# Decode block with a cached attention: value rows from TensorE to GpSimd, key rows from GpSimd to VectorE, and another way to a head's maximum

## The chip, the cores and the metric

The kernel runs on one core of a Trainium2 chip. The metric is the device time of one execution in microseconds; the time of a kernel is the median of several executions. Before the change it is 1319.39 us, the median of three (1319.2 to 1319.57).

## What is computed

One decode step: four sequences (B = 4), one new token each, width D = 512, 32 heads of 128, a key and a value cache of 4096 positions per head and sequence, then a feed-forward layer of width 1792. All is float32.

```
mod = (silu(c) @ w_mod) -> sa, ca, ga, sb, cb, gb          # 6 vectors of 512 per sequence
h = layernorm(x) * (1 + ca) + sa
q = (h @ wq) as [4, 32, 1, 128]
scores = q . k_cache * 128 ** -0.5                          # [4, 32, 1, 4096]
o = softmax(scores) . v_cache
x = x + ga * (o @ wo)
h = layernorm(x) * (1 + cb) + sb
x = x + gb * (silu(h @ w1) @ w2)
```

The two caches hold 268 MB each. They are read once, and nearly all bytes that the kernel moves are theirs.

## The kernel before, in words

The attention is cut into 32 tiles, numbered n = 0 to 31. A tile is four heads (HP = 4) of one sequence: t = n // 4 is the group of heads, b = n % 4 the sequence. Each of the 128 partitions holds 128 consecutive positions of one head (32 partitions per head), so a key tile and a value tile are 128 x 128 x 128 elements each, 8.39 MB: 128 partitions by 128 "rows" (positions) of 128 elements. A tile fills one whole slot of the pool `kv`, which has three slots; the weights that come first (`wm`, `wq`) and last (`wo`, `w12`) use the same three slots. SyncE's queue issues all loads (L86), in the order k1, v0, k2, v1, k3, v2, and so on; a load is issued when its slot is free. With three slots, the load of v(n) goes into the slot of k(n) and waits until the scores of tile n are finished; the load of k(n+2) goes into the slot of v(n-1) and waits until the values of tile n-1 are used up. The order on every engine is the order of the code (a manual schedule).

The loop over n does, for a tile in the middle:

- keys: each key row is multiplied by the query (L283). VectorE does rows 32 to 127 with the query copy `qb`, which lies in PSUM; GpSimd does rows 0 to 31 (`NA` = 32) with the copy `qw` in SBUF, which ScalarE makes (L278). VectorE then sums the 128 elements of each row (L288), its own 96 rows first and GpSimd's 32 after. That gives the 128 x 128 scores `sc`. In tiles 0 and 1 GpSimd has 56 rows (`NL`).
- values of the tile before, n-1: `vmult` and `pv`. GpSimd multiplies rows 0 to 47 (`NP`) by their weights (L331), ScalarE multiplies rows 48 to 55 one at a time (L330, eight instructions), and GpSimd folds these 56 rows (`NV`) to four by four additions (L335, of 28, 12, 8 and 4 rows). TensorE takes rows 56 to 127 unweighted, four rows to a matmul, 18 matmuls, with the weights spread into the stationary operand `pz` (L356). `vsum` (L341) adds GpSimd's four folded rows with one more matmul, read out of the value slot itself.
- maximum: `rowmax` (L292) takes the maximum of each partition's scores; `bmax` (L296) has TensorE transpose it, spread over 128 columns, into PSUM; `negmax` (L301, L302, L304) takes the maximum of each head's 32 columns, multiplies with a mask of -1 (`hn`), and sums. `softexp` has ScalarE take the exponentials (L310), and GpSimd spreads them into `pz` (L316).
- every fourth tile or so VectorE collects a finished group of heads: `gather` (L367, L373), `norm` and `spread`.

On TensorE `vsum(n-1)` stands behind `bmax(n)`. Tiles 30 and 31 have no GpSimd part on their values (`first` gives 0): TensorE takes all 128 rows. At the end come the output projection and the feed-forward, whose weights are loaded behind the last value tile (wo into the slot of k31, w12 into that of v30); small filler matmuls (`busy`) lie between.

Of the kernel before, what the change touches and what calls it, by code (L numbers as in the profile page):

```python
# [9 lines left out]
F32 = mybir.dt.float32  # L10
AF = mybir.ActivationFunctionType
ALU = mybir.AluOpType
AX = mybir.AxisListType
# [4 lines left out]
def kernel(  # L18
# [10 lines left out]
    nc = tc.nc  # L29
    P = 128  # L30
    B, H, S, Dh = kc.shape
# [3 lines left out]
    W = P // G  # L35
    HP = 4
    QW = P // HP
# [6 lines left out]
    JJ = 4  # L44
# [4 lines left out]
    NK = D // P  # L49
    NI = F // P  # L50
    FG = F // G
    NA = 32
    NL = 56
    NV = 56
    NP = 48
    SCALE = 1.0 / math.sqrt(Dh)
    EPS = 1e-5
    N = B * NT
    SLOT = NJ * Dh

    const = ctx.enter_context(tc.tile_pool(name="const", bufs=1))
    kv = ctx.enter_context(tc.tile_pool(name="kv", bufs=3))
    work = ctx.enter_context(tc.tile_pool(name="work", bufs=2))
# [3 lines left out]
    def psum(shape, tag, bufs):  # L67
        return ps.tile(shape, F32, tag=tag, name=tag, bufs=bufs)
# [15 lines left out]
    def fetch(t, src, *cuts):  # L84
        for lo, hi in zip(cuts, cuts[1:]):
            nc.sync.dma_start(t[:, lo:hi], src[:, lo:hi])  # L86

    kt, vt = {}, {}
# [7 lines left out]
    def load_k(n, *cuts):  # L96
        load(kt, kc, "k", n, *cuts)

    def load_v(n):
        load(vt, vc, "v", n)  # L100
# [22 lines left out]
    ident = const.tile([P, P], F32, name="ident")  # L123
# [11 lines left out]
        nc.vector.tensor_scalar(avg[:, g, :], sel, 1.0 / G, None, op0=ALU.mult)  # L135
    hm = const.tile([P, HP], F32, name="hm")
    nc.vector.tensor_reduce(hm, i4, axis=AX.X, op=ALU.add)
    hn = const.tile([P, HP], F32, name="hn")
    nc.vector.tensor_scalar(hn, hm, -1.0, None, op0=ALU.mult)
    jm = const.tile([P, JJ], F32, name="jm")  # L140
    nc.vector.tensor_reduce(jm, ident.rearrange("p (k j) -> p j k", j=JJ), axis=AX.X, op=ALU.add)
    xm = const.tile([P, B], F32, name="xm")
# [15 lines left out]
    hs = const.tile([P, W + E], F32, name="hs")  # L158
# [87 lines left out]
    for k in range(NK):  # L246
        for ch in range(H * Dh // CW):
            i, g = divmod(ch, G)
# [7 lines left out]
    for i in range(2):  # L256
        for u in range(HP):
            o = ZB - QW * u - G * B * i
# [9 lines left out]
    def make_qb(n):  # L268
        if n % B == 0:
            m = work.tile([P, B, Dh], F32, tag="o", name=f"qm{n}", bufs=1)  # L270
            for b in range(B):
                nc.scalar.activation(m[:, b, :], qn, AF.Copy, scale=sel[:, n + b : n + b + 1])  # L272
            p = psum([P, B, Dh], "q", 2)
            nc.tensor.matmul(p, blk.rearrange("p i x -> p (i x)"), m, start=True, stop=True)  # L274
            for b in range(B):
                qb[n + b] = p[:, b, :]
        qw[n] = work.tile([P, Dh], F32, tag="qw", name=f"qw{n}")
        nc.scalar.activation(qw[n], qb[n], AF.Copy)  # L278

    sc, nm, po, rs = {}, {}, {}, {}  # L280

    def mult(eng, src, n, lo, hi):
        eng.tensor_mul(  # L283
            kt[n][:, lo:hi, :], kt[n][:, lo:hi, :], src[n].unsqueeze(1).to_broadcast([P, hi - lo, Dh])
        )

    def red(n, lo, hi):
        nc.vector.tensor_reduce(sc[n][:, lo:hi], kt[n][:, lo:hi, :], axis=AX.X, op=ALU.add)  # L288

    def rowmax(n):  # L290
        nm[n] = work.tile([P, 1], F32, tag="rm", name=f"rm{n}")
        nc.vector.tensor_reduce(nm[n], sc[n], axis=AX.X, op=ALU.max)  # L292

    def bmax(n):
        p = psum([P, P + HP], "mx", 2)
        nc.tensor.transpose(p[:, :P], nm[n].to_broadcast([P, P]), ident)  # L296
        nm[n] = p

    def negmax(n):
        m = nm[n][:, P:]  # L300
        nc.vector.tensor_reduce(m, nm[n][:, :P].rearrange("p (i x) -> p i x", i=HP), axis=AX.X, op=ALU.max)  # L301
        nc.vector.tensor_mul(m, m, hn)  # L302
        nm[n] = work.tile([P, 1], F32, tag="nm", name=f"nm{n}")
        nc.vector.tensor_reduce(nm[n], m, axis=AX.X, op=ALU.add)  # L304

    def softexp(n):
        t, b = divmod(n, B)
        if b == 0:
            rs[t] = work.tile([P, B], F32, tag="rs", name=f"rs{t}")
        nc.scalar.activation(sc[n], sc[n], AF.Exp, bias=nm[n], accum_out=rs[t][:, b : b + 1])  # L310
        for h in range(2):
            f = min(max(first(n) - HG * h, 0), HG)
            m = HG - f
            if not m:
                continue
            nc.gpsimd.tensor_mul(  # L316
                pz[h][:, f * W : HG * W].rearrange("p (g x) -> p g x", g=m)[:, :, E:].rearrange("p g (i j) -> p g i j", i=HP),
                sc[n][:, JJ * (HG * h + f) : HG * JJ * (h + 1)].rearrange("p (g j) -> p g j", j=JJ)
                .unsqueeze(2).to_broadcast([P, m, HP, JJ]),
                hm.unsqueeze(1).unsqueeze(3).to_broadcast([P, m, HP, JJ]),  # L320
            )

    def first(n):
        return NV // JJ if n < N - 2 else 0

    def vmult(n):
        if first(n):
            v = vt[n]
            for j in range(NP, NV):
                nc.scalar.activation(v[:, j, :], v[:, j, :], AF.Copy, scale=sc[n][:, j : j + 1])  # L330
            nc.gpsimd.tensor_mul(  # L331
                v[:, :NP, :], v[:, :NP, :], sc[n][:, :NP].unsqueeze(2).to_broadcast([P, NP, Dh])
            )
            for m, lo in ((28, 28), (12, 16), (8, 8), (JJ, JJ)):
                nc.gpsimd.tensor_add(v[:, :m, :], v[:, :m, :], v[:, lo : lo + m, :])  # L335

    def vsum(n):
        t, b = divmod(n, B)
        q, a = divmod(b, 2)
        o = (1 - a) * E  # L340
        nc.tensor.matmul(  # L341
            po[t, q][0:W, :], hs[:, o : o + W], vt[n][:, :JJ, :].rearrange("p j d -> p (j d)"),
            start=False, stop=a == 1,
        )

    def pv(n):
        t, b = divmod(n, B)
        q, a = divmod(b, 2)
        if a == 0:
            po[t, q] = psum([P, JJ * Dh], "po", 2)  # L350
        f = first(n)
        for j in range(f, NG):
            g = j % G
            h, u = divmod(j, HG)
            o = u * W + (1 - a) * E
            nc.tensor.matmul(  # L356
                po[t, q][W * g : W * (g + 1), :],
                pz[h][:, o : o + W],
                vt[n][:, JJ * j : JJ * (j + 1), :].rearrange("p j d -> p (j d)"),
                start=(a == 0 and j < f + G), stop=(a == 1 and j >= NG - G and (g > 0 or not f)),  # L360
            )
# [25 lines left out]
    def sums(t):  # L387
        p = psum([P, B], "mx", 2)
        if t < TA:
            nc.tensor.matmul(p[W * t : W * (t + 1)], b8.rearrange("p i x -> p (i x)"), rs[t], start=True, stop=True)  # L390
        else:
            nc.tensor.matmul(p, blk.rearrange("p i x -> p (i x)"), rs[t], start=True, stop=True)
        rd[t] = p
# [53 lines left out]
    for n in range(N):  # L447
        t, b = divmod(n, B)
        if n + 1 < N:
            load_k(n + 1)  # L450
        else:
            load_v(n)
        if t and b == 1:
            sums(t - 1)
        sc[n] = work.tile([P, NJ], F32, tag="sc", name=f"sc{n}")
        w, m = (NJ // 2, NL // 2) if n == 0 else (NJ, NL) if n == 1 else (NJ, NA)
        for lo in range(0, NJ, w):
            mult(nc.gpsimd, qw, n, lo, lo + m)
            mult(nc.vector, qb, n, lo + m, lo + w)
            if n + 1 < N and not lo:  # L460
                make_qb(n + 1)
            if n:
                vmult(n - 1)
                pv(n - 1)
            red(n, lo + m, lo + w)
        for lo in range(0, NJ, w):
            red(n, lo, lo + m)
        if n + 1 < N:
            load_v(n)
        else:  # L470
            so = Slot("wo")
            wat, wot = so.take(RA, D), so.take(NT - TA, R, D)
            fetch(so.t, wo, 0, RA * D, SLOT - R * D, SLOT)
            s2 = Slot("w12")
            w1t = s2.take(NK, F)
            w2t = s2.take(NI, D)
            fetch(s2.t, w12, 0, 3 * F, *(NK * F + i * D for i in (0, 5, 8, 10, 11, 12, 13, 14)))
        rowmax(n)
        bmax(n)
        if n and first(n - 1):  # L480
            vsum(n - 1)
        negmax(n)
        softexp(n)
        if b == 3:
            gather(t, 0)
        if n == N - 1:
            sums(t)
            norm(t)
        if t and b == 1:
            gather(t - 1, 1)  # L490
            norm(t - 1)
        if t and b == 2:
            spread(t - 1)
# [25 lines left out]
    for g in range(G):  # L519
        o = g % 2 * P  # L520
# [71 lines left out]
```

## Time and profile before

| | |
|---|---|
| median of three runs | 1319.39 us |
| the profiled execution's own time | 1318.86 us |
| its span, first to last instruction | 1317.0 us |
| bytes read from HBM | 567.30 MB |
| VectorE (DVE) busy | 1045.5 us |
| GpSimd (POOL) busy | 1080.1 us |
| TensorE (PE) matmuls busy | 359.7 us |
| ScalarE (ACT) busy | 125.8 us |
| mean granted TensorE clock | 0.617 of full speed |

The profile is one execution on the chip. A group of instructions is named by its line in the kernel, its engine and operation, and what it writes and reads (partitions x elements); behind the bar stand its busy time, the mean of one in ns, and the engine's idle time just before it with what ended that. The chain of work is followed back from the last instruction to what released each step. A row of the timeline gives start and length in us. "DMA share" is the mean busy share of the core's 16 DMA engines.

### The profile page before, as it was taken

How to read it: one execution, taken by the hardware profiler on the slowest of the kernel's cores; microseconds unless marked ns; L12 is line 12 of the kernel's file. 1: busy time of each engine (PE TensorE's matmuls, PEld its weight loads, DVE VectorE, ACT ScalarE, POOL GpSimd, SP SyncE). 2: the span in 40 equal slices, each digit the busy share in tenths (PEclk: the TensorE clock that was granted, in tenths of full speed). 3: DMA queues.
4: the chain of work that ended last, by engine and by line, in shares of the span. 5: the costliest groups of instructions: out<-in, count | busy, mean ns of one | idle time of the engine just before them, and what ended most of it. 6: DMA issues, size and time to landing. Idle time of an engine off the chain costs nothing.

```text
span 1317.0 us, 5073 instructions
## 1 busy us (share of the span) xinstructions
PE 359.7 (27%) x1756; PEld 95.2 (7%) x1756; DVE 1045.5 (79%) x357; ACT 125.8 (10%) x408; POOL 1080.1 (82%) x257
## 2 busy tenths in 40 slices
PE   3301322221222232122322122132312213221258
PEld 1100000000000000000000000000000000000013
DVE  2597788988878998788898888789887878978762
ACT  1100110010001101011100100000100010000001
POOL 0459888888988888998888899888889888888910
PEclk9856666656666665666665566666556666655669
DMA  9999999999999999999999999999999999999998
GB/s 415 440 420 444 428 435 434 426 442 434 430 440 428 438 435 428 438 434 432 430 442 432 430 439 432 434 434 430 438 432 432 438 432 434 436 432 438 428 426 349
DMA packets 11433, 567.63 MB, mean 431 GB/s; under 512 B 1280, under 2 KB 1296, under 8 KB 2192
## 3 DMA queue, kind: packets, MB, share of 16 engines
q1 hardware_dynamic: 11408, 567.31, 99.6%
q8 instruction: 14, 0.23, 0.1%
q14 instruction: 11, 0.09, 0.0%
HBM read 567.30 MB, written 0.01 MB: 431 GB/s over the span
## 4 chain that ended last, share of the span: by engine, by line
DMA 50%; DVE 27%; POOL 19%; PE 2%; issue 1%; ACT 0%; SPq 0%; DVEq 0%; POOLq 0%
DMA k<-in_A_k_cache_dram 23%; DMA v<-in_A_v_cache_dram 21%; DVE sc L288 16%; DVE k L283 11%; POOL v L335 11%; POOL v L331 8%; DMA w<-in_B_w_dram 3%; DMA wq<-in_A_wq_dram 3%; PE po L341 1%; PE q L249 1%; PE mx L259 0%; ACT qm L272 0%; PE q L274 0%; SPq L86 0%; PE od L378 0%
## 5 line engine op out<-in xcount | busy, mean ns | idle before, releaser
L288 DVE TENSOR_REDUCE sc<-k 128x96 f32<-128x12288 f32 (+3 forms) x66 | 553.1, 8422 | 4.1
L283 DVE TENSOR_TENSOR k<-k,q 128x12288 f32<-128x12288 f32 (+2 forms) x33 | 408.3, 12372 | 183.1 <-DMA k<-in_A_k_cache_dram 168.1
L335 POOL TENSOR_TENSOR v<-v 128x3584 f32<-128x3584 f32 (+1 forms) x120 | 443.8, 3698 | 9.4
L331 POOL TENSOR_TENSOR v<-v,sc 128x6144 f32<-128x6144 f32 x30 | 313.8, 10460 | 103.4 <-DMA v<-in_A_v_cache_dram 103.4
L283 POOL TENSOR_TENSOR k<-k,qw 128x4096 f32<-128x4096 f32 (+2 forms) x33 | 296.4, 8982 | 31.4 <-ACT qw L278 31.4
L356 PE MATMUL po<-v,pz 128*32 128x512 f32 x1208 | 216.3, 839 | 335.6 <-DMA v<-in_A_v_cache_dram 335.6
L341 PE MATMUL po<-v,hs 128*32 128x512 f32 x60 | 57.4, 1061 | 413.8 <-POOL v L335 413.8
L330 ACT ACTIVATE v<-v,sc 128x128 f32<-128x128 f32 x240 | 73.6, 389 | 199.3 <-DMA v<-in_A_v_cache_dram 199.3
L356 PEld LDWEIGHTS po<-v,pz 128*32 128x32 f32 x1208 | 56.1, 148 | 500.8 <-issue 482.3
L296 PE MATMUL mx<-ident,rm 128*128 128x128 f32 x32 | 12.7, 396 | 175.7 <-DVE rm L292 175.7
L278 ACT ACTIVATE qw<-q 128x128 f32<-128x128 f32 x32 | 8.9, 278 | 525.6 <-DVE k L283 424.0
L316 POOL TENSOR_TENSOR pz<-sc,hm 128x32 f32<-128x32 f32 (+1 forms) x64 | 26.7, 438 | 30.4 <-ACT sc L310 30.4
L310 ACT ACTIVATE sc<-sc,nm 128x128 f32<-128x128 f32 x32 | 12.9, 402 | 367.9 <-DVE nm L304 367.9
L341 PEld LDWEIGHTS po<-v,hs 128*32 128x32 f32 x60 | 5.4, 140 | 421.5 <-POOL v L335 421.5
L301 DVE TENSOR_REDUCE mx<-mx 128x4 f32<-128x128 f32 x32 | 9.6, 300 | 17.8 <-PE mx L296 17.8
L367 DVE TENSOR_TENSOR o<-po,jm 128x512 f32<-128x512 f32 x16 | 10.9, 681 | 13.6 <-PE po L356 13.6
L296 PEld LDWEIGHTS mx<-ident,rm 128*128 128x128 f32 x32 | 5.2, 163 | 203.9 <-issue 162.1
L373 DVE TENSOR_REDUCE s<-o 128x128 f32<-128x512 f32 x16 | 16.5, 1034 | 0.6
L274 PE MATMUL q<-qm,blk 128*128 128x512 f32 x16 | 15.6, 1073 | 1.7 <-ACT qm L272 1.7
L200 PE MATMUL q<-wm 128*32 128x512 f32 x48 | 8.9, 668 | 18.9 <-DVE wm L184 18.9
L190 POOL COPY wm<-wm 128x16 f32<-128x16 f32 x1 | 0.2, 212 | 16.0 <-DMA wm<-in_head_dram 16.0
L499 PE MATMUL q<-mod,ident 128*128 128x512 f32 (+2 forms) x24 | 10.7, 554 | 0.0
(114 smaller groups left out, 164.9 us busy)
## 6 DMA issues: line engine op xcount, KB each, us to landing
k<-in_A_k_cache_dram SPq DMA_DIRECT2D x2, 4096.0 KB, 51.1
wm<-in_head_dram SPq DMA_DIRECT2D x1, 6160.0 KB, 17.7
wo<-in_A_wo_dram SPq DMA_DIRECT2D x1, 4096.0 KB, 18.1
wo<-in_A_wo_dram SPq DMA_DIRECT2D x1, 3072.0 KB, 25.0
w<-in_B_w_dram SPq DMA_DIRECT2D x1, 2688.0 KB, 33.1
w<-in_B_w_dram SPq DMA_DIRECT2D x1, 1280.0 KB, 37.3
wo<-in_A_wo_dram SPq DMA_DIRECT2D x1, 1024.0 KB, 27.0
w<-in_B_w_dram SPq DMA_DIRECT2D x4, 256.0 KB, 17.6
```

The source lines that it names most:

```text
L249: nc.tensor.matmul(pq[i][W * g : W * (g + 1), :], hT[:, k, :], wqt[:, k, ch * CW : (ch + 1) * CW], start=k == 0, stop=k == NK - 1,)
L274: nc.tensor.matmul(p, blk.rearrange("p i x -> p (i x)"), m, start=True, stop=True)
L283: eng.tensor_mul(kt[n][:, lo:hi, :], kt[n][:, lo:hi, :], src[n].unsqueeze(1).to_broadcast([P, hi - lo, Dh]))
L288: nc.vector.tensor_reduce(sc[n][:, lo:hi], kt[n][:, lo:hi, :], axis=AX.X, op=ALU.add)
L296: nc.tensor.transpose(p[:, :P], nm[n].to_broadcast([P, P]), ident)
L316: nc.gpsimd.tensor_mul(pz[h][:, f * W : HG * W].rearrange("p (g x) -> p g x", g=m)[:, :, E:].rearrange("p g (i j) -> p g i j", i=HP), sc[n ...
L330: nc.scalar.activation(v[:, j, :], v[:, j, :], AF.Copy, scale=sc[n][:, j : j + 1])
L331: nc.gpsimd.tensor_mul(v[:, :NP, :], v[:, :NP, :], sc[n][:, :NP].unsqueeze(2).to_broadcast([P, NP, Dh]))
L335: nc.gpsimd.tensor_add(v[:, :m, :], v[:, :m, :], v[:, lo : lo + m, :])
L341: nc.tensor.matmul(po[t, q][0:W, :], hs[:, o : o + W], vt[n][:, :JJ, :].rearrange("p j d -> p (j d)"), start=False, stop=a == 1,)
L356: nc.tensor.matmul(po[t, q][W * g : W * (g + 1), :], pz[h][:, o : o + W], vt[n][:, JJ * j : JJ * (j + 1), :].rearrange("p j d -> p (j d)") ...
L373: nc.vector.tensor_reduce(s, o.rearrange("p j d -> p d j"), axis=AX.X, op=ALU.add)
```

## The change

Three things, in one diff.

1. `NV` goes from 56 to 64 and `NP` goes away: GpSimd weighs 64 value rows in one multiplication, ScalarE's eight multiplications are gone, and four additions fold 64 rows as 32, 16, 8 and 4. The last addition writes a tile of its own (`vs`, one buffer), and `vsum` reads that and no longer the value slot. TensorE has 16 matmuls per tile in place of 18. Tile 30 gets 32 rows on GpSimd (`NU`), tile 31 none.
2. `NA` goes from 32 to 8: GpSimd multiplies 8 key rows, VectorE 120, from tile 2 on.
3. `bmax` is gone. `negmax` has VectorE transpose the row maxima in blocks of 32 x 32, take the maximum over 32 columns, and negate it with a `tensor_scalar` of one element per partition, SBUF to SBUF. The mask `hn` is gone.

```diff
-    NA = 32
+    NA = 8
     NL = 56
-    NV = 56
-    NP = 48
+    NV = 64
+    NU = 32
...
-    def bmax(n):
-        p = psum([P, P + HP], "mx", 2)
-        nc.tensor.transpose(p[:, :P], nm[n].to_broadcast([P, P]), ident)
-        nm[n] = p
-
     def negmax(n):
-        m = nm[n][:, P:]
-        nc.vector.tensor_reduce(m, nm[n][:, :P].rearrange("p (i x) -> p i x", i=HP), axis=AX.X, op=ALU.max)
-        nc.vector.tensor_mul(m, m, hn)
-        nm[n] = work.tile([P, 1], F32, tag="nm", name=f"nm{n}")
-        nc.vector.tensor_reduce(nm[n], m, axis=AX.X, op=ALU.add)
+        m = work.tile([P, QW], F32, tag="hx", name=f"hx{n}")
+        nc.vector.transpose(m, nm[n].to_broadcast([P, QW]))
+        nm[n] = work.tile([P, 2], F32, tag="nm", name=f"nm{n}")
+        nc.vector.tensor_reduce(nm[n][:, 0:1], m, axis=AX.X, op=ALU.max)
+        nc.vector.tensor_scalar(nm[n][:, 1:2], nm[n][:, 0:1], -1.0, None, op0=ALU.mult)
...
-        nc.scalar.activation(sc[n], sc[n], AF.Exp, bias=nm[n], accum_out=rs[t][:, b : b + 1])
+        nc.scalar.activation(sc[n], sc[n], AF.Exp, bias=nm[n][:, 1:2], accum_out=rs[t][:, b : b + 1])
...
     def first(n):
-        return NV // JJ if n < N - 2 else 0
+        return (NV if n < N - 2 else NU if n < N - 1 else 0) // JJ
 
     def vmult(n):
-        if first(n):
-            v = vt[n]
-            for j in range(NP, NV):
-                nc.scalar.activation(v[:, j, :], v[:, j, :], AF.Copy, scale=sc[n][:, j : j + 1])
-            nc.gpsimd.tensor_mul(
-                v[:, :NP, :], v[:, :NP, :], sc[n][:, :NP].unsqueeze(2).to_broadcast([P, NP, Dh])
-            )
-            for m, lo in ((28, 28), (12, 16), (8, 8), (JJ, JJ)):
-                nc.gpsimd.tensor_add(v[:, :m, :], v[:, :m, :], v[:, lo : lo + m, :])
+        v, m = vt[n], JJ * first(n)
+        nc.gpsimd.tensor_mul(v[:, :m, :], v[:, :m, :], sc[n][:, :m].unsqueeze(2).to_broadcast([P, m, Dh]))
+        vs[n] = work.tile([P, JJ, Dh], F32, tag="vs", name=f"vs{n}", bufs=1)
+        while m > JJ:
+            m //= 2
+            nc.gpsimd.tensor_add(vs[n] if m == JJ else v[:, :m, :], v[:, :m, :], v[:, m : 2 * m, :])
 
     def vsum(n):
...
-            po[t, q][0:W, :], hs[:, o : o + W], vt[n][:, :JJ, :].rearrange("p j d -> p (j d)"),
+            po[t, q][0:W, :], hs[:, o : o + W], vs[n].rearrange("p j d -> p (j d)"),
...
         rowmax(n)
-        bmax(n)
-        if n and first(n - 1):
+        if n:
             vsum(n - 1)
```

The line numbers of the changed kernel differ: its L281 is L283 of before, L286 is L288, L290 is L292, L309 is L316, L321 is L331, L325 is L335, L331 is L341, L346 is L356.

The order of GpSimd's instructions around the values of tile 6 (`v6`) and the key rows of tile 7 (`k7`); `sc` are scores or weights, `qw` the query. Before:

```order
L316 TENSOR_TENSOR pz0_113<-sc6_598,hm_96 128x2x16
L316 TENSOR_TENSOR pz1_114<-sc6_598,hm_96 128x16x16
L283 TENSOR_TENSOR k7_596<-k7_596,qw7_601 128x4096
L331 TENSOR_TENSOR v6_636<-v6_636,sc6_598 128x6144
L335 TENSOR_TENSOR v6_636<-v6_636 128x3584
L335 TENSOR_TENSOR v6_636<-v6_636 128x1536
L335 TENSOR_TENSOR v6_636<-v6_636 128x1024
L335 TENSOR_TENSOR v6_636<-v6_636 128x512
```

And GpSimd's order at the same place now, with `vs6` as the new tile for the folded rows:

```order
L309 TENSOR_TENSOR pz1_112<-sc6_539,hm_96 128x16x16
L281 TENSOR_TENSOR k7_537<-k7_537,qw7_542 128x1024
L321 TENSOR_TENSOR v6_568<-v6_568,sc6_539 128x8192
L325 TENSOR_TENSOR v6_568<-v6_568 128x4096
L325 TENSOR_TENSOR v6_568<-v6_568 128x2048
L325 TENSOR_TENSOR v6_568<-v6_568 128x1024
L325 TENSOR_TENSOR vs6_598<-v6_568 128x512
```

The small key multiplication stands where the large one stood, the value multiplication and the first two additions are longer, and one of the two spreads into `pz` is gone.

VectorE's order for the scores and the maximum of tile 6, up to the next tile's keys (`mx` lies in PSUM, `od` too, `v`/`oa` belong to the collection of a finished group). Before:

```order
L288 TENSOR_REDUCE sc6_598<-k6_528 128x96
L288 TENSOR_REDUCE sc6_598<-k6_528 128x32
L292 TENSOR_REDUCE rm6_638<-sc6_598 128x1
L301 TENSOR_REDUCE mx_640<-mx_640 128x4
L302 TENSOR_TENSOR mx_640<-mx_640,hn_98 128x4
L304 TENSOR_REDUCE nm6_645<-mx_640 128x1
L416 TENSOR_TENSOR v_650<-od_466,ra_593 32x512
L420 TENSOR_REDUCE oa_130<-v_650 32x64
L283 TENSOR_TENSOR k7_596<-k7_596,q_412 128x12288
```

And VectorE's order there now, with `hx` as the transposed maxima:

```order
L286 TENSOR_REDUCE sc6_539<-k6_480 128x120
L286 TENSOR_REDUCE sc6_539<-k6_480 128x8
L290 TENSOR_REDUCE rm6_570<-sc6_539 128x1
L294 STREAM_TRANSPOSE hx6_573<-rm6_570 128x32
L296 TENSOR_REDUCE nm6_575<-hx6_573 128x1
L297 TENSOR_SCALAR nm6_575<-nm6_575 128x1
L406 TENSOR_TENSOR v_580<-od_429,ra_534 32x512
L410 TENSOR_REDUCE oa_128<-v_580 32x64
L281 TENSOR_TENSOR k7_537<-k7_537,q_386 128x15360
```

Three instructions still stand between the row maxima and the collection, but nothing in them comes from TensorE any more, and the last of them is the `TENSOR_SCALAR` of one element.

More of the change, by code (lines that the diff above doesn't have):

```diff
@@ L137 @@
     nc.vector.tensor_reduce(hm, i4, axis=AX.X, op=ALU.add)
-    hn = const.tile([P, HP], F32, name="hn")
-    nc.vector.tensor_scalar(hn, hm, -1.0, None, op0=ALU.mult)
     jm = const.tile([P, JJ], F32, name="jm")
@@ L278, in make_qb @@
         nc.scalar.activation(qw[n], qb[n], AF.Copy)
-    sc, nm, po, rs = {}, {}, {}, {}
+    sc, nm, po, rs, vs = {}, {}, {}, {}, {}
     def mult(eng, src, n, lo, hi):
```

## The prediction, made blind

> **What bounds the kernel now.** The profile's page comes first: busy time of the engines, the queue's share of the DMA engines, and the shares of the chain that ended last.
>
> ```profile
> PE 359.7 (27%) x1756; PEld 95.2 (7%) x1756; DVE 1045.5 (79%) x357; ACT 125.8 (10%) x408; POOL 1080.1 (82%) x257
> q1 hardware_dynamic: 11408, 567.31, 99.6%
> DMA 50%; DVE 27%; POOL 19%; PE 2%; issue 1%; ACT 0%; SPq 0%; DVEq 0%; POOLq 0%
> ```
>
> The chain gives half to DMA and nearly half to VectorE and GpSimd, as if their work paced the kernel. The queue's row says otherwise: packets occupied the 16 DMA engines for 99.6% of the span, and only 0.4% of 1317.0 us, 5.3 us, was empty. So I read one turn of the chain in order of time, and three tiles in the windows (columns: length, busy time and instructions of PE, PEld, DVE, ACT, POOL, then TensorE clock, DMA share, GB/s).
>
> ```profile
> 571.62 27.38 DMA v<-in_A_v_cache_dram
> 599.13 10.47 POOL v L331
> ...
> 624.75 1.93 PE po L341 x2
> 626.74 30.76 DMA k<-in_A_k_cache_dram
> 657.58 12.97 DVE k L283
> 670.66 17.29 DVE sc L288 x2
> 687.97 27.43 DMA v<-in_A_v_cache_dram
> ```
> ```profile
> 1121.84:1237.62 115.78, 28.39 (x123) 7.61 (x123) 96.04 (x28) 9.89 (x34) 104.36 (x25) 0.59 1.00 435
> ```
>
> The turn is a slot's life: load values, use them, load keys, use them. A load "takes" 27 to 31 us there, but three tiles move six loads of 8.39 MB in 115.78 us, 19.3 us for each at 435 GB/s with a DMA share of 1.00. So a load spends 8 to 11 us queued behind the one before. A tile lasts 38.6 us because two loads last that long. The compute pieces in the chain only decide how early a load joins the queue. The spare time is best seen in the timeline: a value load's issue beside the landing of the key load ahead of it, and a value landing.
>
> ```profile
> 726.61 0.33 SPq L86 DMA_DIRECT2D v<-in_A_v_cache_dram  x1
> ```
> ```profile
> 734.82 12.96 DVE L283 TENSOR_TENSOR k<-k,q 128x12288 f32<-128x12288 f32 x1 [4.45 <-DMA k<-in_A_k_cache_dram]
> ```
> ```profile
> 637.73 10.46 POOL L331 TENSOR_TENSOR v<-v,sc 128x6144 f32<-128x6144 f32 x1 [3.46 <-DMA v<-in_A_v_cache_dram]
> ```
>
> The value load joins at 726.61 and the keys ahead of it land by 734.82: a lead of 8.2 us. The key load of 626.74 (chain above) joins 11.0 us before the values ahead of it land, by 637.73. VectorE waits 4.45 us for its keys in this tile, and 168.1 us over the 30 tiles (group row below), 5.6 on average; GpSimd waits 3.46.
>
> **The change part by part.** The groups, shapes kept apart:
>
> ```profile
> L283 DVE TENSOR_TENSOR k<-k,q 128x12288 f32<-128x12288 f32 x30 | 388.6, 12954 | 168.1 <-DMA k<-in_A_k_cache_dram 168.1
> L288 DVE TENSOR_REDUCE sc<-k 128x96 f32<-128x12288 f32 x30 | 388.6, 12953 | 4.0
> L331 POOL TENSOR_TENSOR v<-v,sc 128x6144 f32<-128x6144 f32 x30 | 313.8, 10460 | 103.4 <-DMA v<-in_A_v_cache_dram 103.4
> L283 POOL TENSOR_TENSOR k<-k,qw 128x4096 f32<-128x4096 f32 x30 | 265.5, 8852 | 0.0
> L335 POOL TENSOR_TENSOR v<-v 128x3584 f32<-128x3584 f32 x30 | 232.0, 7733 | 2.4
> L288 DVE TENSOR_REDUCE sc<-k 128x32 f32<-128x4096 f32 x30 | 132.3, 4409 | 0.0
> L335 POOL TENSOR_TENSOR v<-v 128x1536 f32<-128x1536 f32 x30 | 103.0, 3434 | 2.4
> L335 POOL TENSOR_TENSOR v<-v 128x1024 f32<-128x1024 f32 x30 | 70.7, 2356 | 2.4
> L335 POOL TENSOR_TENSOR v<-v 128x512 f32<-128x512 f32 x30 | 38.1, 1269 | 2.4
> L316 POOL TENSOR_TENSOR pz<-sc,hm 128x256 f32<-128x256 f32 x34 | 20.8, 614 | 16.2 <-ACT sc L310 16.2
> ```
>
> *Keys.* VectorE's product grows by 24 rows: 12.95 us x 120/96 = 16.19, so +3.24 us per tile, +97 us over 30 tiles. The sums cover 128 rows as before: 12.95 x 120/96 + 4.41 / 4 = 17.29 against 17.36. The key slot comes free 3.2 us later, and the value load's lead falls from 8.2 to 5.0 us. What hides it is the key load still in the queue ahead. The lead needed is an issue's start-up; the nearest row is the output's whole transfer, 1.8 us from issue to landing (quoted under the ends), so between 0 and 1.8 us. 5.0 covers it. Were the cover gone, each tile would pay the missing part.
>
> *Values on GpSimd.* The product: 10.46 x 64/48 = 13.95 us. The additions: 7.73 x 32/28 = 8.84, 3.43 x 16/12 = 4.58, 2.36 and 1.27, together 17.05. From landing to the last addition that is 31.0 us and four gaps of 0.07 (the chain's steps), 31.3. Before, the next key load was issued 27.6 us after the values' start (599.13 to 626.74), TensorE's 1.93 included; now the folded rows leave the slot, and that matmul no longer holds it. The key load joins 3.7 us later, with a lead of 11.0 - 3.7 = 7.3 us. A wide product no trace shows: at the additions' pace (7.73 / 3584 an element) it would be 17.7 us, and the lead still 3.5. I take 13.95, the same operation's row.
>
> *GpSimd in all.* Keys 8.85 / 4 = 2.21, values 31.0, one spread 0.61: 33.8 us, against 8.85 + 10.46 + 14.79 + 0.61 and the small second spread, 34.7 without that. It gets about 1 us shorter and keeps waiting for its values. With the wide product at its upper bound it has 37.6, still under 38.6. Eight ScalarE multiplications and two matmuls per tile go from engines busy 10% and 27%; worth nothing.
>
> *The maximum.* Five rows of VectorE's timeline, with what GpSimd runs meanwhile:
>
> ```profile
> 919.23 7.73 POOL L335 TENSOR_TENSOR v<-v 128x3584 f32<-128x3584 f32 x1
> ```
> ```profile
> 920.68 0.30 DVE L301 TENSOR_REDUCE mx<-mx 128x4 f32<-128x128 f32 x1 [0.63 <-PE mx L296]
> 921.02 0.17 DVE L302 TENSOR_TENSOR mx<-mx,hn 128x4 f32<-128x4 f32 x1
> 921.22 0.16 DVE L304 TENSOR_REDUCE nm<-mx 128x1 f32<-128x4 f32 x1
> 921.30 0.34 DVE L423 TENSOR_SCALAR on<-od,rd 128x128 f32<-128x128 f32 x1
> 921.68 0.31 DVE L427 STREAM_TRANSPOSE ot<-on 128x128 f32<-128x128 f32 x1
> ```
>
> The old way costs 0.63 of waiting and 0.63 of work. The new one: a transpose of 32 columns, at most the 0.31 of 128; a reduction between 0.16 and 0.30; a negation near 0.16. That is 0.7 against 1.26, about 0.5 us saved. VectorE's wait for keys in the tightest tile becomes 4.45 - 3.24 + 0.5 = 1.7 us. It stays positive, so VectorE stays ahead of DMA, though it is now the tightest engine. The negation's upper end is a rival, below.
>
> *Ends.* Rows of SyncE's timeline, the output's issue (us to landing last), TensorE's start on the last two value tiles, and the chain's last load:
>
> ```profile
> 0.74 0.38 SPq L118 DMA_DIRECT2D wm<-in_head_dram  x1
> ...
> 1268.01 1.28 SPq L86 DMA_DIRECT2D wo<-in_A_wo_dram  x3
> ```
> ```profile
> out_dram<-end SPq DMA_DIRECT2D x1, 8.0 KB, 1.8
> ```
> ```profile
> 1257.00 9.15 PE L356 MATMUL po<-v,pz 128*32 128x512 f32 x64 [11.11 <-DMA v<-in_A_v_cache_dram]
> ...
> 1276.53 4.50 PE L356 MATMUL po<-v,pz 128*32 128x512 f32 x20 [4.54 <-DMA v<-in_A_v_cache_dram]
> ```
> ```profile
> 1302.47 10.75 DMA w<-in_B_w_dram
> ```
>
> The output weights' load would be issued at 1268.0 + 3.2 = 1271.2 us, 5.3 before the last values land at 1276.5. Tile 30's 32 rows cost GpSimd 6.97 (half of 13.95), 8.21 of additions (4.58, 2.36, 1.27) and gaps, 15.4 us, from 1257.0 to 1272.4; the feed-forward weights wait for that slot, but stand behind 8.39 MB of output weights, 19.3 us, in any case. The end is the landing of their last piece at 1302.47 + 10.75 = 1313.2 us, and 1317.0 - 1313.2 = 3.8 us of last steps that the change doesn't touch. The first load starts at 0.74 as before.
>
> *Sum.* Every added microsecond lies under the queue: 0 on the span. 1317.0 + 0 gives 1317.0, and 1318.9 for the profiled execution (1318.86, span plus 1.86); the median of the runs is 0.53 above that, so 1319.4.
>
> **The rivals.** *The negation waits for GpSimd.* At the start of the trace, VectorE's copies and scalings from SBUF to SBUF look like this beside two GpSimd fills:
>
> ```profile
> 1.39 1.01 POOL L157 MEMSET pz<- 128x528 f32 x2
> ```
> ```profile
> 1.92 0.50 DVE L132 COPY selb<-sel 128x4 f32<-128x4 f32 x1
> 2.00 0.51 DVE L135 TENSOR_SCALAR avg<-sel 128x32 f32<-128x32 f32 x4
> ...
> 3.02 0.16 DVE L143 COPY xm<-sel 128x4 f32<-128x4 f32 x1
> ```
>
> The copy at 1.92 lasts 0.50 and ends at 2.42, where the fills end (2.40); the same size takes 0.16 later, with GpSimd idle. The scalings end just behind. Reductions, the transpose, and a scaling that reads PSUM don't stretch (rows of 920.68 to 921.68, inside GpSimd's addition of 7.73 us). The new negation is a scaling from SBUF to SBUF, and it comes some 34.4 us after the keys' landing (33.5 and the maximum), 15.1 after the values': inside the 8.84 us addition, which runs from 14.0 to 22.9. If it waits, it waits 7.8 us, more than the 1.7 to spare. The next tile then starts late, its value load joins an empty queue, and GpSimd's addition, for which the negation after next waits, comes late too. That cycle spans two tiles: product and sums 33.5, start-up up to 1.8, load 19.3, GpSimd's product and first addition 22.9, collecting 0.7 (921.30 and 921.68), 78.2 us or 39.1 a tile. That is 0.5 over 38.6, times 30: 15 us, so about 1334 (with no start-up to pay it would be 38.2, and covered again). It decides as soon as the wait exceeds 1.7 us. For it: the stretched rows. Against it: those had 4 and 32 elements per partition, this has one, which no row shows beside a busy GpSimd; nor does the trace show that the instruction has to be of the kind that waits. [...] I give the wait 1 in 10, and 2 in 100 more to any other stretch of VectorE by over 1.7 us a tile, with a like price.
>
> *The DMA engines gain.* If anything that now slows packets went away (TensorE and ScalarE read less), or the ends shortened, the limit is the 5.3 us of empty time: 1314. At a DMA share of 1.00 and 435 GB/s in the middle I see nothing to gain; the ends aren't touched. 3 in 100.
>
> **How the numbers follow.** No change has 0.85, slower 0.12, faster 0.03; 0.2%, 2.6 us, is about what a measurement of this kernel can tell from no change. The likeliest time is 1319.4. Its range: above, one start-up of 1.8 us exposed, to 1321.2; below, three times the 0.5 by which the profiled run already lies under the median, to 1317.9. That holds about 0.85, so the rivals at 1314 and 1334 stay outside.
>
> **What would show it.** In the profile after: DMA share 1.00 in the middle and 99.6% in the queue's row; VectorE's products near 16.2 us and its wait for keys near 2 us; GpSimd's product near 14 and first addition 8.8; value loads landing some 24 us after issue, not 27. VectorE's busy time rises to some 1130 us without the span moving. Wrong would be: a negation of several us, a wait of VectorE for keys that is gone, or a DMA share under 0.99 in the middle.

## The result and the profile after

| | before | after |
|---|---|---|
| median of seven runs each, same chip | 1319.35 us | 1323.0 us |
| lowest and highest | 1318.99, 1319.57 | 1322.53, 1328.66 |
| profiled execution, its span | 1318.86, 1317.0 us | 1322.73, 1320.9 us |

The ratio of the means is 1.0038, with a 95% interval of 1.0028 to 1.0048: slower, by 3.65 us in the median and 5.0 us in the mean, and with more scatter upward. The forecast was no change.

The page of the changed kernel, in the order in which the prediction read that of before (span, busy time, the queue's share, the chain):

```profile
span 1320.9 us, 4423 instructions
...
PE 324.7 (25%) x1590; PEld 82.7 (6%) x1590; DVE 1138.7 (86%) x356; ACT 52.3 (4%) x168; POOL 1062.9 (80%) x231
...
q1 hardware_dynamic: 11408, 567.31, 99.5%
...
DMA 45%; DVE 30%; POOL 23%; PE 1%; issue 1%; ACT 0%; DVEq 0%; POOLq 0%; SPq 0%
```

The engines did what was worked out: VectorE is busy 93 us longer, GpSimd 17 shorter, and the queue still fills the DMA engines for 99.5% of a span that is 3.9 us longer. The groups of the changed kernel, shapes kept apart (busy us, mean ns, idle time ahead):

```profile
L281 DVE TENSOR_TENSOR k<-k,q 128x15360 f32<-128x15360 f32 x30 | 484.6, 16154 | 97.9 <-DMA k<-in_A_k_cache_dram 97.9
L286 DVE TENSOR_REDUCE sc<-k 128x120 f32<-128x15360 f32 x30 | 484.6, 16153 | 3.5 <-DVE k L281 0.5
L321 POOL TENSOR_TENSOR v<-v,sc 128x8192 f32<-128x8192 f32 x30 | 416.5, 13884 | 138.3 <-DMA v<-in_A_v_cache_dram 138.3
L325 POOL TENSOR_TENSOR v<-v 128x4096 f32<-128x4096 f32 x30 | 265.1, 8836 | 2.4
L281 POOL TENSOR_TENSOR k<-k,qw 128x1024 f32<-128x1024 f32 x30 | 70.7, 2357 | 0.0
L294 DVE STREAM_TRANSPOSE hx<-rm 128x32 f32<-128x32 f32 x32 | 6.8, 211 | 1.1
L296 DVE TENSOR_REDUCE nm<-hx 128x1 f32<-128x32 f32 x32 | 6.0, 186 | 1.1
L297 DVE TENSOR_SCALAR nm<-nm 128x1 f32<-128x1 f32 x32 | 4.9, 154 | 1.1
```

VectorE still waits for its keys, 97.9 us over 30 tiles, 3.3 on average, and GpSimd for its values, 4.6: neither has become the bound. One load shows the new lead: the issue of a value load, and VectorE's start on the keys ahead of it.

```profile
731.54 0.33 SPq L86 DMA_DIRECT2D v<-in_A_v_cache_dram  x1
```
```profile
736.68 16.15 DVE L281 TENSOR_TENSOR k<-k,q 128x15360 f32<-128x15360 f32 x1 [2.06 <-DMA k<-in_A_k_cache_dram]
```

The lead is 5.1 us, and VectorE still waits 2.06 us; in the same tile of the kernel before they were 8.2 and 4.45. So the extra time should lie in the loads themselves. Three tiles are too few to see it, since stretches of three tiles within the kernel before already lie between 115.78 and 116.35 us. Here are 27 tiles, from VectorE's start on the keys of tile 3 to its start on those of tile 30, in the windows of the kernel after and of the one before:

```profile
154.86:1201.76 1046.90, 229.74 (x972) 53.28 (x972) 958.56 (x247) 34.54 (x123) 911.40 (x190) 0.57 1.00 433
```
```profile
154.38:1199.06 1044.68, 261.35 (x1107) 64.12 (x1107) 874.34 (x247) 100.70 (x339) 940.44 (x217) 0.59 1.00 434
```

The stretch has the same loads at the same DMA share of 1.00, and it takes 1046.90 us in place of 1044.68: 2.2 us, or 0.08 a tile. Of the span's other 1.7 us, 0.5 lie ahead of the stretch and 1.2 behind it. The queue was full in both and took longer for the same bytes, so its packets should be slower. A share cannot show that, since a slow packet counts as busy (1.00 in both); the rate does (433 against 434 GB/s), but coarsely. The trace keeps the duration of every DMA packet. The row of one partition in a slot is one packet of 64 KB: 64 loads of 128 rows, 8,192 packets. Before, 7,874 take 2418 ns, and the mean is 2419.4. After, only 829 take 2418; 4,031 take 2421 and 1,562 take 2428; the mean is 2424.9. Shared among 16 engines they are 512 for each: 5.5 ns x 512 = 2.8 us. Of that, 0.8 us is in a few long packets, over 2440 ns (68 of them; 42 before), and 2.0 us in all the ordinary ones.

### The profile page after: what moved, and what is told of

Its sections match the earlier page's. It is cut to its first block, busy times and chain, and to the rows that moved or that the text cites. A ratio compares the mean times of both kernels' runs of the same rounds, so it can differ in the third digit from the quotient of the medians.

```text
span 1320.9 us, 4423 instructions
## 1 busy us (share of the span) xinstructions
PE 324.7 (25%) x1590; PEld 82.7 (6%) x1590; DVE 1138.7 (86%) x356; ACT 52.3 (4%) x168; POOL 1062.9 (80%) x231
## 3 DMA queue, kind: packets, MB, share of 16 engines
q1 hardware_dynamic: 11408, 567.31, 99.5%
## 4 chain that ended last, share of the span: by engine, by line
DMA 45%; DVE 30%; POOL 23%; PE 1%; issue 1%; ACT 0%; DVEq 0%; POOLq 0%; SPq 0%
DMA k<-in_A_k_cache_dram 20%; DMA v<-in_A_v_cache_dram 19%; DVE sc L286 16%; DVE k L281 14%; POOL v L325 12%; POOL v L321 11%; DMA w<-in_B_w_dram 3%; DMA wq<-in_A_wq_dram 3%; POOL vs L325 1%; PE q L247 1%; PE mx L257 0%; ACT qm L270 0%; PE q L272 0%; DVE s L363 0%; DVE o L357 0%
## 5 line engine op out<-in xcount | busy, mean ns | idle before, releaser
L281 DVE TENSOR_TENSOR k<-k,q 128x15360 f32<-128x15360 f32 (+2 forms) x33 | 504.3, 15281 | 111.4 <-DMA k<-in_A_k_cache_dram 97.9
L286 DVE TENSOR_REDUCE sc<-k 128x120 f32<-128x15360 f32 (+3 forms) x66 | 553.1, 8422 | 3.6 <-DVE k L281 0.5
L321 POOL TENSOR_TENSOR v<-v,sc 128x8192 f32<-128x8192 f32 (+1 forms) x31 | 423.6, 13663 | 142.6 <-DMA v<-in_A_v_cache_dram 142.6
L325 POOL TENSOR_TENSOR v<-v 128x2048 f32<-128x2048 f32 (+2 forms) x92 | 478.4, 5200 | 7.2
L331 PE MATMUL po<-vs,hs 128*32 128x512 f32 x62 | 59.4, 1061 | 771.1 <-POOL vs L325 771.1
L346 PE MATMUL po<-v,pz 128*32 128x512 f32 x1072 | 190.7, 878 | 195.5 <-DMA v<-in_A_v_cache_dram 195.5
L281 POOL TENSOR_TENSOR k<-k,qw 128x1024 f32<-128x1024 f32 (+2 forms) x33 | 101.6, 3078 | 31.7 <-ACT qw L276 31.5
L346 PEld LDWEIGHTS po<-v,pz 128*32 128x32 f32 x1072 | 48.3, 154 | 341.4 <-issue 341.4
L331 PEld LDWEIGHTS po<-vs,hs 128*32 128x32 f32 x62 | 5.6, 141 | 801.0 <-POOL vs L325 801.0
L325 POOL TENSOR_TENSOR vs<-v 128x512 f32<-128x512 f32 x31 | 39.3, 1269 | 2.4
L309 POOL TENSOR_TENSOR pz<-sc,hm 128x256 f32<-128x256 f32 (+1 forms) x34 | 20.6, 607 | 13.5 <-ACT sc L303 13.5
L198 PE MATMUL q<-wm 128*32 128x512 f32 x48 | 10.0, 721 | 18.7 <-DVE wm L182 18.7
L270 ACT ACTIVATE qm<-qn,sel 128x128 f32<-128x128 f32 x32 | 10.2, 389 | 4.9 <-DVE oa L410 4.8
```

What stands on the lines that cost most here:

```text
L281: eng.tensor_mul(kt[n][:, lo:hi, :], kt[n][:, lo:hi, :], src[n].unsqueeze(1).to_broadcast([P, hi - lo, Dh]))
L309: nc.gpsimd.tensor_mul(pz[h][:, f * W : HG * W].rearrange("p (g x) -> p g x", g=m)[:, :, E:].rearrange("p g (i j) -> p g i j", i=HP), sc[n ...
L321: nc.gpsimd.tensor_mul(v[:, :m, :], v[:, :m, :], sc[n][:, :m].unsqueeze(2).to_broadcast([P, m, Dh]))
L325: nc.gpsimd.tensor_add(vs[n] if m == JJ else v[:, :m, :], v[:, :m, :], v[:, m : 2 * m, :])
L331: nc.tensor.matmul(po[t, q][0:W, :], hs[:, o : o + W], vs[n].rearrange("p j d -> p (j d)"), start=False, stop=a == 1,)
L346: nc.tensor.matmul(po[t, q][W * g : W * (g + 1), :], pz[h][:, o : o + W], vt[n][:, JJ * j : JJ * (j + 1), :].rearrange("p j d -> p (j d)") ...
```

## The experiments

What was different about the packets? The built programs give a candidate. The mask `hn`, 16 bytes in each partition, is a constant that lies ahead of the three slots, and it takes 32 bytes there. Without it the slots start at byte 19168 of a partition, 224 beyond a multiple of 256; with it they start at 19200, a multiple of 256. **The theory of the address** (A in the expectations below): that shift makes the packets slower. **The theory of the lead** (B): the value load, which now joins the queue 5.1 us before the keys ahead of it have landed, joins too late. Rivals: the negation or another new instruction holds VectorE (C); the change of GpSimd's and VectorE's work on the keys, the values and the maximum costs something that the page doesn't show (D); or any move of the slots costs.

**The address.** First the changed kernel with the slots put back (e1), and the kernel before with nothing changed but their place (e2). The unused tile stands among the constants, ahead of the slots.

```diff
+    const.tile([P, 8], F32, name="gap")
     jm = const.tile([P, JJ], F32, name="jm")
```

That is e1, in the changed kernel: 32 bytes, slots at 19200.

> The changed kernel with one unused constant of 32 bytes per partition where the removed mask stood, so that the three 64 KB slots start at byte 19200 (a multiple of 256) again, as in the kernel before, and not at 19168. Theory A (the slots' start address sets how long a 64 KB packet takes; the change moved it by 32 bytes): the time returns to 1319.4 us (ratio 1.000), VectorE still 1139 us busy. Theory B (VectorE's later release of the key slot makes the queue run short): nothing in that is undone, the time stays near 1323 (ratio 1.003 to 1.004). Theory C (the negation or another new instruction holds VectorE): also stays near 1323.

Measured: 1320.73 us (1319.68 to 1322.8), 1.0011 times before (1.0002 to 1.0019); before was 1319.22 on that chip. With the slots back, 7,870 packets take 2418 ns again, and its 27 tiles are nearly back, with all else as in the changed kernel:

```profile
154.68:1199.76 1045.08, 230.54 (x972) 53.52 (x972) 958.56 (x247) 34.56 (x123) 911.65 (x190) 0.57 1.00 434
```

VectorE's 958.56 us is that of the changed kernel to the digit; the length is 0.4 us over that of the kernel before. The time lies between what theory A and theory B gave: most of the loss is gone, and 1.5 us of it stay.

In e2 the same line stands in the kernel before with `[P, 56]`: 224 bytes, slots at 19424, which is again 224 beyond a multiple of 256.

> The kernel before, with one unused constant of 224 bytes per partition, so that the slots start at byte 19424, 224 beyond a multiple of 256 as in the changed kernel; no instruction differs. Theory A: 1322.5 to 1323.5 us (ratio 1.0025 to 1.004). Theories B and C: 1319.4 (ratio 1.000), since the leads and the maximum are those of before.

Measured: 1322.79 us (1322.41 to 1323.25), 1.0027 (1.0016 to 1.0037). One unused tile makes the old kernel as slow as the new one. Its 27 tiles:

```profile
155.03:1202.87 1047.84, 262.46 (x1107) 64.46 (x1107) 874.37 (x247) 100.67 (x339) 940.65 (x217) 0.59 1.00 433
```

1047.84 us in place of 1044.68, 0.12 a tile. The leads are untouched (its value loads land 27.6 us after issue, 27.4 before), and so are the engines: VectorE is busy 874.37 us there and 874.34 before.

Which addresses are slow? Four more kernels differ from before only in the size of that tile: `[P, 16]`, `[P, 32]`, `[P, 64]` and `[P, 8]`, that is 64, 128, 256 and 32 bytes.

> The kernel before with an unused constant of 64 bytes: slots at byte 19264, a multiple of 64 but not of 128 or 256. Theory A leaves open what the address must be a multiple of: if 64 is enough, 1319.4 us (ratio 1.000); if it must be 256, about 1322 to 1323 (ratio 1.002 to 1.004). Theories B and C: 1319.4.

> The kernel before with an unused constant of 128 bytes: slots at byte 19328, a multiple of 128 but not of 256. Theory A: 1319.4 us (ratio 1.000) if 128 is enough, 1322 to 1323 (ratio 1.002 to 1.004) if it must be 256. Theories B and C: 1319.4.

> The kernel before with an unused constant of 256 bytes: slots at byte 19456, 256 further than before. Theory A, with 256 as the unit: 1319.1 us, ratio 1.000. If any move from 19200 costs something (the distance to other tiles, say): 1321.5 to 1323, ratio 1.002 to 1.003.

> The kernel before with an unused constant of 32 bytes: slots at byte 19232, an odd multiple of 32. Theory A, if a start that is no multiple of 64 costs more than one that is: as e2, 1322.5 to 1323 us, ratio 1.0025 to 1.003. If only the multiple of 256 counts: as e3 and e4, 1321.7 to 1322, ratio 1.002.

Before was 1319.22 us on the chip of e2, e3 and e4, and 1319.14 on that of e11 and e12.

| run | slots start at | beyond a multiple of 256 | median, us | ratio (95%) | mean packet, ns |
|---|---|---|---|---|---|
| before | 19200 | 0 | see above | | 2419.4 |
| e11 | 19456 | 0 | 1319.25 | 1.0001 (0.9992 to 1.0009) | 2419.1 |
| e4 | 19328 | 128 | 1321.9 | 1.002 (1.0011 to 1.0029) | 2422.7 |
| e3 | 19264 | 64 | 1321.89 | 1.0019 (1.001 to 1.0028) | 2422.9 |
| e12 | 19232 | 32 | 1322.58 | 1.0026 (1.0016 to 1.0035) | 2423.7 |
| e2 | 19424 | 224 | 1322.79 | 1.0027 (1.0016 to 1.0037) | 2423.8 |

A move by 256 bytes costs nothing (e11), so it isn't the move. Off a multiple of 256 it costs 2.7 us, and at an odd multiple of 32 it costs 3.4 to 3.6. Within these runs the distance from the boundary below isn't what counts: 32 and 224 cost the same, and so do 64 and 128.

The weights lie in the same slots, in shorter rows, and there the cost went by the packet and not by the byte. A packet of 4 KB takes 159.0 ns in the kernel before and in e11, and 161.6 to 162.1 in the other four; one of 8 KB takes 309.0 against 313.2 to 314.6; an ordinary one of 64 KB 2418 against 2421.5 to 2422.5. That is 3 to 6 ns each time, 0.2% of a 64 KB row but 2% of a 4 KB row. The packets of the first load (`wm`, 48 KB) don't show it: 1820 ns in 89 of the 128 before and in 90 in the changed kernel.

**The lead.** What is left in e1 should hang on how early the value load joins. Two edits take the key part apart: e5 has only `NA = 8` in the kernel before, slots at 19200; e6 is e1 with `NA = 16`, so that it keeps the whole value part and the new maximum, with a value load that joins 1 us earlier.

```diff
-    NA = 32
+    NA = 8
```

> The kernel before with NA = 8 alone: VectorE takes 120 key rows, values and maximum as before, slots at byte 19200. The value load's lead falls from 8.2 to some 5.0 us, the key load's stays at 11. Theory B (what is left of the loss with the address repaired, 1.5 us of e1, comes from the value load joining the queue too late: its first packets are stretched on the engines that are ahead): 1320.5 to 1321 us, ratio 1.001, and scattered as e1. Theory D (the rest comes from the value part or the maximum, on GpSimd or VectorE): 1319.2, ratio 1.000.

Measured: 1319.71 us (1319.3 to 1321.04), 1.0006 (0.9997 to 1.0015), before 1319.04. Less than was expected, and not told from no change; but three of its eleven runs lie at 1320.58 to 1321.04, where no run of the kernel before lay (at most 1319.62).

> The changed kernel with the address repaired and NA = 16: GpSimd takes 16 key rows, VectorE 112; value load's lead about 6.1 us in place of 5.0, GpSimd 2.2 us busier per tile and still under the tile's 38.6. Theory B: half or more of the rest is gone, 1319.3 to 1320 us, ratio 1.000 to 1.0005. Theory D: as e1, 1320.7, ratio 1.001.

Measured: 1319.12 us (1318.59 to 1319.52), 1.0 (0.9992 to 1.0009). The page of e6:

```profile
span 1316.9 us, 4423 instructions
...
PE 323.2 (25%) x1590; PEld 82.7 (6%) x1590; DVE 1106.7 (84%) x356; ACT 52.3 (4%) x168; POOL 1127.3 (86%) x231
...
q1 hardware_dynamic: 11408, 567.31, 99.6%
```

So 64 value rows on GpSimd, the new maximum and 61 us more on VectorE together cost nothing, and the rival about the values and the maximum falls. What remains is the last 8 key rows: 1 us of lead, and 32 us of VectorE's work.

To vary the lead alone, four kernels hold the value load back in the kernel before: `load_v(n)` moves behind `softexp(n)`, and a ScalarE copy of some rows of the key slot onto themselves keeps the slot busy. VectorE, GpSimd and TensorE keep their instructions. The number of rows is 1 (e7), 8 (e9), 14 (e10) or 24 (e8):

```diff
-        if n + 1 < N:
+        if n < 2:
             load_v(n)
...
         softexp(n)
+        if 2 <= n < N - 1:
+            nc.scalar.activation(kt[n][:, :1, :], kt[n][:, :1, :], AF.Copy)
+            load_v(n)
```

> The kernel before, in which ScalarE copies one key row onto itself after the exponentials of each tile from 2 to 30; the value load waits for that. No work moves between engines; only the key slot is held some 2.7 us longer, so the value load's lead falls from 8.2 to about 5.5 us. Theory B: 1320 to 1321 us, ratio 1.0005 to 1.0015. Theory D: 1319.2, ratio 1.000.

> The kernel before, with eight key rows copied onto themselves by ScalarE before the value load: its lead falls to about 5.1 us, that of the changed kernel, with all the arithmetic and all other leads of before. Theory B (only the lead counts, with a knee near 5 us): 1319.5 to 1320.7 us, ratio 1.0003 to 1.0012, scattered upward. Theory D (what e1 and e5 lose comes from VectorE's longer product): 1319.1, ratio 1.000.

> The same with 14 rows: lead about 4.5 us, between e9 and e8. Theory B: between them, 1321 to 1332 us, ratio 1.0015 to 1.010. [...]

> The same with 24 key rows copied onto themselves (some 2.6 us more): the value load's lead falls to about 3 us. Theory B: clearly slower than e7, 1322 to 1330 us, ratio 1.002 to 1.008, since the engines that are ahead now run dry. Theory D: 1319.2, ratio 1.000.

The lead is the time from a value load's issue to the landing of the keys ahead of it, from the trace, over tiles 2 on. The 16 engines don't finish a load together, so it is given to the last and to the first of them. The loss is the median less that of before on the same chip. The last two columns are of the one run that was profiled, and that is not the median run: in e9 it was the slowest of eleven, in e5 the fastest. The seam is where the packets of the key load end and those of the value load begin; long packets at the seam are those over 2440 ns that start within 6 us of a value load's issue.

| run | lead to the last, mean (least) | to the first, mean (least) | loss, us | ratio (95%) | loss of the profiled run, us | its long packets: all, at the seam |
|---|---|---|---|---|---|---|
| before | 8.2 (8.1) | 6.0 (5.1) | | | | 42, 3 |
| e6 | 6.1 (5.7) | 3.8 (2.6) | 0.1 | 1.0 (0.9992 to 1.0009) | -0.2 | 28, 3 |
| e7 | 5.8 (5.6) | 3.5 (2.8) | 0.2 | 1.0001 (0.9992 to 1.001) | 0.3 | 41, 13 |
| e9 | 5.1 (4.9) | 2.9 (1.6) | 0.3 | 1.0004 (0.9995 to 1.0013) | 2.0 | 98, 74 |
| e5 | 5.0 (4.7) | 2.9 (2.2) | 0.7 | 1.0006 (0.9997 to 1.0015) | 0.3 | 50, 28 |
| e1 | 5.0 (4.5) | 3.0 (2.2) | 1.5 | 1.0011 (1.0002 to 1.0019) | 1.1 | 100, 51 |
| e10 | 4.7 (4.2) | 2.5 (1.3) | 6.5 | 1.0049 (1.0036 to 1.0061) | 7.7 | 303, 194 |
| e8 | 3.9 (3.4) | 1.9 (0.9) | 18.7 | 1.0141 (1.0127 to 1.0155) | 16.9 | 821, 478 |

The time is flat down to 5.8 us, begins to scatter at 5.0 and is steep below. e7 was expected to lose 1 to 2 us and lost nothing that can be told: moving the load into another place of the code costs nothing by itself. Nor does holding it for the 1.04 us that 8 rows take (an estimate from 1.68 us for 14 rows in e10 and 2.75 for 24 in e8), outside the scatter: nine of e9's eleven runs took 1319.15 to 1319.51 us, the other two 1320.98 and 1321.17. The medians of e10 and e8 are 1325.63 and 1337.73 us; e8 lost more than was expected, so the bend is sharper than I took it. It lies where the first engine is some 2 to 3 us from running dry, and not only where one is dry: in e10 the first engine always had 1.3 us or more left, 2.5 on average. (The prediction's own bounds for a start-up were 0 to 1.8 us.) The long packets at the seam come with the loss: what they take beyond an ordinary packet, shared among the 16 engines, is 0.1 us before, 1.1 in e1, 1.5 in e9, 4.9 in e10 and 11.5 in e8, the greater part of what these runs lost. One load of e8: SyncE's issue of the values, ScalarE's copy ahead of it, and the starts of the tile then in VectorE and of the next.

```profile
896.89 0.33 SPq L86 DMA_DIRECT2D v<-in_A_v_cache_dram  x1
```
```profile
894.12 2.75 ACT L485 ACTIVATE k<-k 128x3072 f32<-128x3072 f32 x1
```
```profile
900.78 12.95 DVE L283 TENSOR_TENSOR k<-k,q 128x12288 f32<-128x12288 f32 x1 [5.00 <-DMA k<-in_A_k_cache_dram]
...
940.14 12.95 DVE L283 TENSOR_TENSOR k<-k,q 128x12288 f32<-128x12288 f32 x1 [6.89 <-DMA k<-in_A_k_cache_dram]
```

The load is issued 3.9 us before the keys land, and the tile lasts 39.36 us, 0.7 more than the mean of before (1044.68 / 27 = 38.69), though VectorE still waits for its keys at both ends. In the packet records 16 packets that start from 898.60 to 901.71, just at the seam, are longer than 2440 ns, by up to 1.6 us more than an ordinary one. ScalarE's copy had ended by then (896.87), so it isn't the copy that slows them. e1 has such a group too, four packets that start 2.4 to 3.0 us after an issue at 305.12, up to 1.3 us longer. The 27 tiles of e8, in the windows:

```profile
155.15:1214.78 1059.63, 259.26 (x1107) 63.71 (x1107) 874.72 (x246) 170.84 (x366) 940.80 (x217) 0.60 1.00 428
```

Even here, where 27 tiles take 15 us more than before, the share reads 1.00; the rate falls from 434 to 428 GB/s.

**The account.** The address alone has a ratio of 1.0027 (e2), and what is left in the changed kernel with the address repaired is 1.0011 (e1), which e6 to e10 lay mainly to the lead: together 1.0038, as measured. In medians they are 3.6 and 1.5 us against 3.65, because four of the seven runs of the changed kernel lie at e2's level (1322.53 to 1323.0) and the other three at 1324.46, 1326.19 and 1328.66: the lead shows as scatter.

What stays open:

- Why packets at a seam are stretched.
- Whether e1 really loses more than e5 and e9 at the same lead. The three intervals overlap, but e1's fastest run, 1319.68, is slower than nine of e9's eleven. In e1's profiled run the long packets at the seam account for 1.0 of the 1.1 us lost; why e1 should lose in all its runs what e9 loses in two of eleven isn't shown, and VectorE's longer product, which e5 has too, is not ruled out.
- The slowest run of the changed kernel, 1328.66. Its granted TensorE clock was 0.554, that of the other six 0.589 to 0.601; whether that has to do with its time isn't shown, since it wasn't the profiled run.
- Why the span of e2 is 4.0 us longer than that of before, when all packets of the queue, those of the weights included, take only 2.7 us more on each engine.

No version was found that beats both kernels; e6, the best of the changed ones, equals before.

## Why the prediction was wrong, point by point

**The sum failed.** The sentence "Every added microsecond lies under the queue: 0 on the span" holds for the added work, but it took the queue's own pace, 19.3 us for a load, as given. The change altered that pace in a line that the prediction had costed at nothing: "the mask `hn` is gone" was weighed as VectorE's instruction only, not as 32 bytes of memory ahead of the slots. That is +3.6 us (e2). The built program shows the shift without a run (the slots' start is no longer a multiple of 256); that it has a price, only the runs show.

**The lead failed in size.** "Between 0 and 1.8 us ... 5.0 covers it": the lead came out as forecast (value loads land 24.4 us after issue; 5.1 us of lead), but the needed lead is between 5 and 6 us (5.8 cost nothing in e7, 5.1 scattered in e9, 4.7 cost 6.5 us in e10), not below 1.8. The small output transfer, alone at the end, was a poor neighbour for a load that has to follow another on 16 engines without a seam; and the last landing was the wrong mark, because the first engine is 2 us ahead of it (a lead of 6.0 against 8.2 us before, 3.0 against 5.0 in e1). The +1.5 us left in e1 are laid mainly to that. The issue to landing rows, before and after, for values and keys:

```profile
v<-in_A_v_cache_dram SPq DMA_DIRECT2D x32, 27.4
...
k<-in_A_k_cache_dram SPq DMA_DIRECT2D x31, 30.3
```
```profile
v<-in_A_v_cache_dram SPq DMA_DIRECT2D x32, 24.4
...
k<-in_A_k_cache_dram SPq DMA_DIRECT2D x31, 26.7
```

**The bound was read rightly, the tell was not.** DMA bounds both kernels. But "DMA share 1.00 in the middle and 99.6%" was to show that nothing is lost, and it stood at 1.00 and 99.5% while the profiled run took 3.9 us more. The time of many tiles and the duration of a packet tell it.

**VectorE, GpSimd and the values were right.** The product came to 16.15 us (16.19 forecast), the value product to 13.88 (13.95), its four additions to 16.99 (17.05), the key lead to 7.4 (7.3), GpSimd's tile to 33.8 (33.8), VectorE's wait in the tile shown to 2.06 (1.7). e6 shows that this part costs nothing, with 112 key rows on VectorE in place of 120.

**The maximum was right, and its rival didn't come.** The line view of the negation (least, median, most in ns; first and last start):

```profile
L297 DVE TENSOR_SCALAR nm<-nm x32: 153/154/156, 78.1 to 1274.8; 128x1 f32<-128x1 f32 x32
```

All 32 take 153 to 156 ns, though 29 of them run wholly inside an 8.84 us addition of GpSimd. That one element would be spared was an estimate of the author's: a scaling of one element beside a busy GpSimd stood in no row of before.

**The ends** moved a little more than worked out: the output weights' load is issued at 1275.27, 4.0 us ahead of the last values' landing at 1279.3 in place of 5.3. The last steps after the last landing still take 3.8 us.

**The range** ended at "one start-up of 1.8 us exposed", once in the whole kernel, and no rival between 1321 and 1334 had a mechanism: none asked what would change the load itself.

## What to carry to other kernels

Where DMA is the bound at a share of 1.00, ask of every edit whether it moves the buffers that DMA writes: a constant added or dropped ahead of them shifts their start, and here a start off a multiple of 256 bytes cost 0.2 to 0.27% of the whole kernel. The price was 3 to 6 ns for a packet of 4, 8 or 64 KB, so shorter rows lost a larger share (2% of 4 KB, 0.2% of 64 KB). Count the lead of a load from the first engine that runs dry, and keep some microseconds in hand: here 5.8 us to the last landing cost nothing and 4.7 cost 6.5 us. Watch the time of many tiles and of a packet, not the busy share, which counts a slow packet as a busy one (1.00 in e8, where 27 tiles took 15 us more).

## What the runs showed of the hardware that was not expected

- A 64 KB packet into SBUF took 2418 ns where the row started at a multiple of 256 bytes (7,874 of 8,192 packets before, 8,030 in e11). At 64 beyond one it mostly took 2420 (3,908 in e3) or 2427 (1,428), at 128 it was spread over 2418, 2422 and 2426 (1,911, 2,107 and 1,214 in e4), at an odd multiple of 32 mostly 2421 or 2428 (4,430 and 1,733 in e2, 4,430 and 1,726 in e12).
- Of two loads of 8.39 MB in one queue, the second followed without a loss when it was issued 5.8 us or more before the first one's last landing (e6, e7); at 5.0 to 5.1 some runs lost 1 to 2 us (e5, e9), and at 3.9 packets at the seam lasted up to 1.9 us longer while the engines counted as busy (a share of 1.00 over 27 tiles of e8).
- The transpose of 128 x 32 took 211 ns and the single-element scaling 154 ns beside a busy GpSimd (31 of 32 each ran inside an instruction of GpSimd); neither waited for it (211 to 213 and 153 to 156 ns over all 32).
